# Polysketch attention with a routed two-layer expert network: more products of zeros at the start, and last output tiles in one plain transfer per queue

## The chip, the cores and the metric

The kernel runs on one core of a Trainium2 chip. Five engines work side by side: TensorE (PE in the profile; PEld is its weight load), VectorE (DVE), ScalarE (ACT), GpSimd (POOL) and SyncE (SP). SP issues most transfers, ACT and POOL some; sixteen DMA engines carry them. An SPq or ACTq row of the timeline is the issuing alone, not the transfer. The metric is the time of one execution in microseconds on the device; lower is better.

## The reference, cut to what matters

Two stages follow each other. The attention has 4 batches, 4 heads, 1088 positions and 32 elements a head. The expert network has 4352 tokens of 128, 8 experts with 1024 hidden elements, and two experts per token.

```python
a, b = S1 @ x, S2 @ x                     # 8 sketches each, for x = q and x = k
phi(x) = outer(a, b)                      # 64 features per position and head
kv = phi(k).T @ v;  z = phi(k).sum(0)
attn = phi(q) @ kv / (phi(q) @ z + 1e-6)  # [4, 1088, 4 heads * 32] = tokens x
noisy = x @ w_gate + log(1 + exp(x @ w_noise)) * noise
top2  = the two largest of 8, softmax weights
out[t] = sum over the token's two experts e of weight * (relu(x[t] @ w1[e]) @ w2[e])
```

## The kernel before, in words

**An order that is written out.** The kernel first makes a list of jobs: each has the engines that may run it, what it reads and writes, and a function that emits its instructions. `PLACES` is the order in which the jobs are emitted, `ENGINES` the engine of each, by its number. Each engine, SP's queue among them, takes its instructions in that order, so a waiting one holds up what is behind it. `HOLDS` ties a group of transfers to a scatter that must come first. `ZEROS` names the jobs ahead of which TensorE multiplies zeros: the number is how many products of 512 columns in bf16 (the last may be shorter). They write to a tile that nobody reads (`idle`, L471). Their operand is in fact a constant of ones; the text keeps the name.

**The first batch** (L626 and on). The matrices S are taken apart (L591 to L603) and turned (L568). Keys and queries are turned on VectorE (L614), multiplied by the sketches (L631, of 64 columns; L634, of 128), taken out of PSUM by ACT, and their outer products are made by VectorE or POOL (L666). When all tiles of keys are there, 72 products give kv (L748); from it come tokens, logits, routing and one-hot columns for the first experts.

**Routing.** For each call of the router a batch's tokens are weighed and scattered by POOL (L1084) into lists per expert in DRAM. With each row goes its pair number, 2 * token + choice, from the table `pid`, which `numbers` fills with iotas on POOL (L543 to L552) and L1047 copies next to the rows.

**The expert stage** (`block`). For each block of 128 or 256 rows of an expert, rows are fetched, turned, multiplied by w1 (L1195), rectified (L1203 on ACT, L1201 on VectorE), multiplied by w2 (L1210) and scattered to `pairs` in DRAM by their pair number (L1238). It begins near 37 us and lasts to the end; sketches and routing of later batches are put among it. The last two blocks are not scattered: their rows are given to the tokens by products with a matrix of ones and zeros, `spread` (L1219, L1228), which leaves sums in two PSUM banks, `late_acc`.

**The end** (`sums`, `in_tiles`). For each batch both rows of a token are loaded from `pairs` (`pr`), added on VectorE (L1268) and stored. A batch but the last has tokens in order on the partitions. In the last one the numbering is that of the tokens' places in the tiles: a partition holds position 32 * strip + t, a column is one of 9 tiles. The load is in that order as well, and the store has to undo it. Columns 0 to 3 are loaded and stored on SP before the last blocks are done. For columns 4 to 7 and for tile 8 the bank is added (L1274) before the store. `in_tiles` makes the targets: for columns below 8 there are two, one for each pair of strips, with extents [2 strips][32 t][columns][128]; partitions are 64 for each. Columns 4 to 7 are added and stored in two halves of two columns each, each half on SP and ACT. Tile 8 has two stores of 32 rows. `pr` and `o` have one buffer each. After the last store each engine reads `flag` and branches (L1484, L1486), to a part for lists that are too long, which isn't entered; then SP waits for all transfers.

Of the kernel before, what the change touches and what calls it, by code (L numbers as in the profile page):

```python
# [1518 lines left out]
```

## Time and profile before

| | |
|---|---|
| median of 3 runs | 352.35 us (350.09, 352.35, 353.89) |
| the profiled execution's own time | 354.55 us |
| its span, first to last instruction | 352.7 us |
| mean granted TensorE clock | 0.983 |
| PE busy | 333.4 us (95%), 2844 products |
| DVE / ACT / POOL busy | 176.6 (50%) / 121.9 (35%) / 237.5 (67%) |
| moved by DMA | 42.82 MB, mean 121 GB/s |

The page cuts the span into 40 slices of 8.8 us; a digit is the busy share in tenths. TensorE is at 9 from the second slice to the 38th with one 8, at 2 in the 39th and 0 in the last. The chain that ended last is empty on this page, so the end is read from the timeline. Line numbers are those of the kernel before; L356 and L349 are helpers that issue all plain transfers and all copies, so their operands tell them apart.

### The profile page before, as it was taken

To read this page: it belongs to the slowest core of one execution; us is meant where nothing else is said; L and a number is where in the kernel's file an instruction comes from. 1 tells how busy PE (TensorE), PEld (TensorE's weight loads), DVE (VectorE), ACT (ScalarE), POOL (GpSimd) and SP (SyncE) were. 2 spreads that over 40 slices of the span, in tenths; PEclk is the share of its full clock that TensorE was granted. 3 is DMA by queue.
4 is the path that set the end of the run, shared out by engine and by line. 5 is a ranking of instruction groups with operands and counts; after the bars stand their busy time and mean duration, and the time that the engine had idled before them with its cause. 6 is when DMAs were issued, how large, how long until landed. Compare 5 with 4: busy or idle time off the path is not lost.

```text
span 352.7 us, 8086 instructions
## 1 busy us (share of the span) xinstructions
PE 333.4 (95%) x2844; PEld 317.6 (90%) x2844; DVE 176.6 (50%) x659; ACT 121.9 (35%) x325; POOL 237.5 (67%) x386
## 2 busy tenths in 40 slices
PE   8999899999999999999999999999999999999920
PEld 4986899999999999999999999999999999999920
DVE  4548887875927675543766522443323333334120
ACT  1237767743455432614122453111112221222300
POOL 7434586986497897396858698893886788646100
PEclk9999999999999999999999999999999999999985
DMA  7728996953475664555324371142343151535510
GB/s 205 236 75 222 253 336 197 267 170 82 98 163 120 119 167 101 72 110 90 74 55 89 58 195 41 41 71 65 62 82 103 62 113 45 144 118 147 139 37 31
DMA packets 91656, 42.82 MB, mean 121 GB/s; under 512 B 67105, under 2 KB 85154, under 8 KB 91612
## 3 DMA queue, kind: packets, MB, share of 16 engines
q1 hardware_dynamic: 86872, 33.24, 42.0%
q0 software_dynamic: 4544, 8.89, 7.1%
q8 instruction: 23, 0.38, 0.5%
q14 instruction: 21, 0.17, 0.2%
q10 hardware_dynamic: 196, 0.15, 0.1%
HBM read 26.27 MB, written 16.17 MB: 120 GB/s over the span
## 4 chain that ended last, share of the span: by engine, by line


## 5 line engine op out<-in xcount | busy, mean ns | idle before, releaser
L1210 PE MATMUL acc<-w2s,h 128*128 128x128 f32 x1152 | 145.5, 276 | 0.0
L1195 PE MATMUL hp<-bT,w1s 128*128 128x128 f32 (+1 forms) x896 | 144.7, 306 | 0.4 <-ACT bT L349 0.4
L1210 PEld LDWEIGHTS acc<-w2s,h 128*128 128x128 f32 x1152 | 139.8, 192 | 2.5
L1195 PEld LDWEIGHTS hp<-bT,w1s 128*128 128x128 f32 x896 | 121.7, 191 | 5.5 <-ACT bT L349 0.5
L1203 ACT ACTIVATE h<-hp 128x512 f32<-128x512 f32 x100 | 59.5, 596 | 134.1 <-PE hp L1195 121.1
L1084 POOL DMA_INDIRECT xs<-xg,to x72 | 71.4, 991 | 36.1 <-issue 13.9
L1238 POOL DMA_INDIRECT pairs<-y,mine x70 | 68.9, 985 | 36.6 <-issue 10.5
L904 POOL MEMSET step<- 1x512 f32 x142 | 73.0, 514 | 0.0
L1201 DVE TENSOR_SCALAR h<-hp 128x512 f32<-128x512 f32 x44 | 30.3, 688 | 67.1 <-PE hp L1195 60.8
L349 ACT COPY y<-acc 128x128 f32<-128x128 f32 x46 | 11.9, 263 | 39.4 <-PE acc L1210 37.4
L1185 DVE STREAM_TRANSPOSE bT<-xb 128x128 f32<-128x128 f32 (+1 forms) x48 | 16.3, 345 | 8.9 <-PE hp L1195 5.2
L1056 ACT ACTIVATE xg<-x,g 128x128 f32<-128x128 f32 x57 | 18.5, 394 | 2.0 <-DVE g L1010 2.0
L349 DVE COPY y<-acc 128x128 f32<-128x128 f32 x24 | 6.8, 285 | 19.8 <-PE acc L1210 11.8
L810 PE MATMUL bank<-kvw,pT 128*128 128x98 f32 x128 | 16.5, 273 | 0.0
L810 PEld LDWEIGHTS bank<-kvw,pT 128*128 128x128 f32 x128 | 15.5, 192 | 0.1
L1268 DVE TENSOR_TENSOR o<-pr 128x512 f32<-128x512 f32 (+1 forms) x12 | 6.5, 552 | 11.7 <-DMA pr<-pairs 11.0
L666 POOL TENSOR_TENSOR phq<-ab 128x512 f32<-128x512 f32 (+1 forms) x5 | 5.3, 1067 | 8.8 <-DVE ab L648 8.8
L634 PE MATMUL bank<-sk,qTs 128*128 128x128 f32 x64 | 10.2, 300 | 0.0
L634 PEld LDWEIGHTS bank<-sk,qTs 128*128 128x128 f32 x64 | 9.1, 213 | 0.2 <-issue 0.2
L666 DVE TENSOR_TENSOR phq<-ab 128x512 f32<-128x512 f32 (+1 forms) x13 | 8.1, 620 | 0.1
L471 PE MATMUL turn<-const-bfloat16-1.0 128*128 128x512 bf16 (+2 forms) x22 | 7.2, 482 | 0.9 <-PEq L1502 0.9
L648 DVE TENSOR_TENSOR ab<-bank,lo 128x256 f32<-128x256 f32 (+2 forms) x17 | 6.4, 383 | 2.8 <-ACT lo L349 2.4
(182 smaller groups left out, 291.6 us busy)
## 6 DMA issues: line engine op xcount, KB each, us to landing
w1s<-in_moe_w_dram SPq DMA_DIRECT2D x8, 512.0 KB
w2s<-in_moe_w_dram SPq DMA_DIRECT2D x8, 512.0 KB
pr<-pairs SPq DMA_DIRECT2D x8, 512.0 KB
kq<-in_k_dram SPq DMA_DIRECT2D x4, 544.0 KB
kq<-in_q_dram SPq DMA_DIRECT2D x4, 544.0 KB
vld<-in_v_dram SPq DMA_DIRECT2D x16, 128.0 KB
xb<-xs SPq DMA_DIRECT2D x128, 16.0 KB
there<-phq SPq DMA_DIRECT2D x16, 128.0 KB
```

Of the source, the lines that this page charges most:

```text
L349: A.copy(o, i) if e == "ACT" else V.tensor_copy(o, i)
L634: T.matmul(ps.t[rows, 2 * W * i:2 * W * i + 2 * W], lhsT=lhsT, rhs=sk[:].rearrange("p c h x -> p (c h x)"), start=True, stop=True)
L810: T.matmul(ps2.t[:, c0:c0 + 2 * YW], lhsT=pT.t[:, at + P * (2 * i + a):at + P * (2 * i + a) + P], rhs=kvw.t[:, a, :], start=True, stop=True)
L904: job.fill = G.memset(step[:], 0.0)
L1056: A.activation(out=xg.t[:, i, c, 0:D], in_=x.t[:, c, :], func=AF.Copy, scale=B_["g"].t[:, i, c:c + 1])
L1084: ins = G.indirect_dma_start(out=xs[:], in_=xg.t[rows, i, t, :], in_offset=None, out_offset=bass.IndirectOffsetOnAxis(ap=to.t[rows, i, t:t ...
L1185: add("DVE", vec(P * n), lambda _: V.transpose(bT.t[:, 0:P * n], flat()), r=[xb], w=[bT], prio=TOP + u)
L1195: T.matmul(hp.t[:, P * n * i:P * n * (i + 1)], lhsT=w1s[:, e, P * (js * g + i):P * (js * g + i + 1)], rhs=bT.t[:, 0:P * n], start=True, st ...
L1201: V.tensor_scalar_max(h.t[:], hp.t[:], 0.0)
L1203: A.activation(out=h.t[:], in_=hp.t[:], func=AF.Relu)
L1210: T.matmul(acc.t[:, D * c:D * c + D], lhsT=h.t[:, P * (n * i + c):P * (n * i + c + 1)], rhs=w2s[:, e, j, :], start=(j == 0 and c == 0), st ...
L1238: ins = G.indirect_dma_start(out=pairs[:], in_=y.t[:], in_offset=None, out_offset=bass.IndirectOffsetOnAxis(ap=numbers_of[w].t[:, e, c:c + ...
```

## The change

Five things are edited, and with them the whole written order.

1. `ZEROS`: 4.5 products instead of 1.9 ahead of the first sketch; one product more ahead of the first product of queries with kv in the second router call. The 7.6 at the very start and the 12 stay (the job numbers move by one).
2. `numbers` no longer fills the last batch; `last_numbers` does, in twelve iotas. In columns 0 to 7 the number is now 8 * t + 2 * strip + choice plus the column's base, so a partition of the loaded sums is 4 * t + strip. In tile 8 it is 4 * t + 2 * strip + choice.
3. `in_tiles` gives targets with extents [16 t][4 strips][columns * 128] for columns below 8, two of them, of 64 partitions each; tile 8 has one target of 64 rows.
4. `sums` adds the bank once and stores each target once; the halves are gone. The products that give the last blocks' rows to columns 0 to 3 of the bank are one job instead of two.
5. `PLACES`, `ENGINES` and `HOLDS` are new. TensorE's own order is nearly the same (1.1 places of shift on average); on SP, ACT and VectorE jobs move by 7 to 14 places on average, and about 50 jobs change from VectorE to ACT or the other way. Near the start: the last query sketch comes ahead of the key products; the blank block `pad` is written early on POOL instead of after the query products; the transfers of the second batch and the weights are reordered, with the second weights of expert 0 seventh among the sixteen weight loads instead of second. `last_numbers` stands among the scatters of batch 2. At the end, SP's order is: the two stores of columns 0 to 3, the load of columns 4 to 7, the load of tile 8, a store of batch 2, the store of columns 4 to 7 (with ACT), the store of tile 8.

```diff
-HOLDS = {'clear5': (1, 4, 0), 'clear6': (8, 0), 'w2_7': (0, 1, 1), 'zeros': (5, 7, 0)}
+HOLDS = {'clear6': (1, 2, 1), 'v3': (1, 2, 1)}
...
-ZEROS = {43: 7.6, 49: 1.9, 152: 12}
+ZEROS = {44: 7.6, 50: 4.5, 153: 12, 222: 1}
@@ -549,8 +549,17 @@
                     if l < 2:
                         G.iota(pid[rows, i, 0:B - 1, C], pattern=[[2 * S, B - 1]], base=2 * (32 + l) + i,
                                channel_multiplier=2 * TN)
-                G.iota(pid[:, i, B - 1, :], pattern=[[2 * P, C + 1]], base=2 * S * (B - 1) + i, channel_multiplier=2)
-        pool_job(2.7, 15, numbers, ["pid"])
+        pool_job(2.5, 15, numbers, [("pid", 0)])
+
+        def last_numbers():
+            for i in range(2):
+                for l in range(4):
+                    rows = slice(32 * l, 32 * l + 32)
+                    G.iota(pid[rows, i, B - 1, 0:C], pattern=[[2 * P, C]], base=2 * S * (B - 1) + 2 * l + i, channel_multiplier=8)
+                    if l < 2:
+                        G.iota(pid[rows, i, B - 1, C:C + 1], pattern=[[2 * P, 1]], base=2 * (S * (B - 1) + P * C) + 2 * l + i,
+                               channel_multiplier=4)
+        pool_job(2.2, 250, last_numbers, [("pid", 1)], [("pid", 0)])
         pool_job(3.0, 26, lambda: limits(1, NW + 1), [("limits", 1)], ["base"])
         add("DVE", 0.3, lambda e: (V.tensor_copy(starts[:, 0, :], base[:]), V.memset(over[:], -1.0)),
             r=["base"], w=[("starts", 0), "over"], prio=45, port=1)
@@ -1045,7 +1054,7 @@
         indexed = dve(0.2 + 2 * vec(16 * n), index, ["first", "row"], ["f2", "at", "to"], late)
         xg, to = B_["xg"], B_["to"]
         pool_job(gps(18) + 0.1, prio, lambda: G.tensor_copy(xg.t[:, :, 0:n, D:XW].bitcast(I32), pid[:, :, b, t0:t0 + n].unsqueeze(3)),
-                 [(xg, 9)], ["pid"])
+                 [(xg, 9)], [("pid", b // (B - 1))])
         for i in range(2):
             for c0 in range(0, n, 3):
                 c1 = min(n, c0 + 3)
@@ -1222,13 +1231,13 @@
             add(EV, either(D), lambda en: copy(en, y[:], acc.t[:, 0:D]), r=[acc], w=[("late", late)], prio=TOP + u)
 
             behind_it = []
-            for cs in ((4,), (0, 1), (2, 3)):
+            for cs in ((4,), (0, 1, 2, 3)):
                 def given(_, cs=cs):
                     for c in cs:
                         T.matmul(late_acc[c // 4].t[:, D * (c % 4):D * (c % 4) + D], lhsT=spread.t[:, P * c:P * c + P], rhs=y[:],
                                  start=(late == 0 and c in (0, 4)), stop=(late == LATE - 1), skip_group_check=True)
                 behind_it = [add("PE", len(cs) * mm(D), given, lat=0.15, r=[spread, ("late", late)],
-                                 w=[(late_acc[cs[0] // 4], cs[0] % 4 // 2)], prio=p0 + 60, after=behind_it)]
+                                 w=[late_acc[cs[0] // 4]], prio=p0 + 60, after=behind_it)]
             return
         for c in range(n):
             y = new("y")
@@ -1268,18 +1277,13 @@
             add("DVE", vec(P * c), lambda e, t=t, o=o, rows=rows, c=c: V.tensor_tensor(
                 out=o.t[rows, 0:c, :], in0=t.t[rows, 0:c, 0, :], in1=t.t[rows, 0:c, 1, :], op=ALU.add),
                 r=[t], w=[o], prio=prio, port=1)
-            halves = [(0, c)] if bank is None or c == 1 else [(0, c // 2), (c // 2, c)]
-            for half, (c0, c1) in enumerate(halves):
-                if bank is not None:
-                    add("DVE", vec(P * (c1 - c0)), lambda e, o=o, rows=rows, c0=c0, c1=c1, bank=bank: V.tensor_tensor(
-                        out=o.t[rows, c0:c1, :], in0=o.t[rows, c0:c1, :],
-                        in1=bank.t[rows, c0 * D:c1 * D].rearrange("p (c d) -> p c d", d=D), op=ALU.add),
-                        r=[(bank, half)], w=[(o, half)], prio=prio)
-                for i, (d_, part) in enumerate(dsts):
-                    dma(queues[i % len(queues)],
-                        lambda d_=d_, c0=c0, c1=c1, cut=len(halves) > 1: d_[:, :, c0:c1, :] if cut else d_,
-                        lambda o=o, part=part, c0=c0, c1=c1: o.t[part, c0:c1, :], [(o, half)], [("out", (b, at, half, i))], prio,
-                        size=600.0 * (c1 - c0) * (part.stop - part.start))
+            if bank is not None:
+                add("DVE", vec(P * c), lambda e, o=o, rows=rows, c=c, bank=bank: V.tensor_tensor(
+                    out=o.t[rows, 0:c, :], in0=o.t[rows, 0:c, :],
+                    in1=bank.t[rows, 0:c * D].rearrange("p (c d) -> p c d", d=D), op=ALU.add), r=[bank], w=[o], prio=prio)
+            for i, (d_, part) in enumerate(dsts):
+                dma(queues[i % len(queues)], lambda d_=d_: d_, lambda o=o, part=part, c=c: o.t[part, 0:c, :], [o], [("out", (b, at, i))],
+                    prio, size=600.0 * c * (part.stop - part.start))
 
     def whole(b):
         r0 = S * b
@@ -1297,10 +1301,9 @@
         src = pairs_t[r0 + P * c0:r0 + P * c1].rearrange("(c p) k d -> p c k d", p=P)
         dst = out[r0:r0 + S, :].rearrange("(t n) d -> t n d", n=TN)
         if c0 == C:
-            return ([(src[0:HB], slice(0, HB))], [(dst[:, 32 + l:33 + l], slice(32 * l, 32 * l + 32)) for l in range(2)], 1,
-                    late_acc[1])
-        dst = dst[:, 0:32].rearrange("t (l c) d -> l t c d", l=4)[:, :, c0:c1, :]
-        return ([(src, slice(0, P))], [(dst[2 * l:2 * l + 2], slice(64 * l, 64 * l + 64)) for l in range(2)], c1 - c0,
+            return [(src[0:HB], slice(0, HB))], [(dst[:, 32:TN, :].unsqueeze(2), slice(0, HB))], 1, late_acc[1]
+        dst = dst[:, 0:32, :].rearrange("t (l c) d -> t l c d", c=C)[:, :, c0:c1, :]
+        return ([(src, slice(0, P))], [(dst[16 * i:16 * i + 16], slice(64 * i, 64 * i + 64)) for i in range(2)], c1 - c0,
                 late_acc[0] if c0 else None)
 
     late_acc = [new("bank"), new("bank")]
```

## Rows read from the trace of the kernel before

**Rows 1.** The page, part 2: busy tenths of PE and DMA in 40 slices.

```profile
PE   8999899999999999999999999999999999999920
...
DMA  7728996953475664555324371142343151535510
```

**Rows 2.** Windows: busy us by engine, granted clock, DMA share, GB/s.

```profile
40.00:60.00 20.00, 20.00 (x235) 19.13 (x234) 15.89 (x65) 14.77 (x43) 15.14 (x18) 1.00 1.00 278
250.00:300.00 50.00, 50.00 (x341) 46.92 (x340) 16.24 (x40) 10.16 (x22) 40.23 (x61) 1.00 0.31 78
```

**Rows 3.** Timeline from 330 us: start us, us, engine, line, operation, count.

```profile
329.63 0.69 DVE L1268 TENSOR_TENSOR o<-pr 128x512 f32<-128x512 f32 x1 [4.56 <-DMA pr<-pairs]
...
330.35 1.19 SPq L356 DMA_DIRECT2D out_dram<-o  x2
...
331.85 1.24 SPq L356 DMA_DIRECT2D pr<-pairs  x2
...
336.37 1.38 PE L1228 MATMUL bank<-late_y,blocks 128*128 128x128 f32 x10 [0.35 <-ACT late_y L349]
340.68 0.88 DVE L1268 TENSOR_TENSOR o<-pr 128x512 f32<-128x512 f32 x2 [5.85 <-DMA pr<-pairs]
341.67 0.94 DVE L1274 TENSOR_TENSOR o<-o,bank 64x128 f32<-64x128 f32 x3
341.97 1.64 SPq L356 DMA_DIRECT2D out_dram<-o  x3
341.98 1.91 ACTq L356 DMA_DIRECT2D out_dram<-o  x3
```

**Rows 4.** Windows over stretches near the end.

```profile
324.00:325.00 1.00, 1.00 (x11) 1.00 (x10) 0.86 (x4) 0.00 (x1) 0.34 (x1) 1.00 0.54 201
334.00:335.00 1.00, 1.00 (x12) 1.00 (x11) 0.55 (x1) 0.00 (x0) 0.00 (x0) 1.00 0.97 338
...
347.00:350.00 3.00, 0.00 (x0) 0.00 (x0) 0.00 (x0) 0.00 (x0) 0.00 (x0) 0.50 0.14 48
```

**Rows 5.** Lines 1484 and 1486: duration ns min/median/max, first and last start.

```profile
L1484 SPq TENSOR_LOAD <-flag x1: 1563/1563/1563, 343.7 to 343.7; - x1
...
L1486 SPq EVENT_SEMAPHORE  x8: 17/17/17, 345.8 to 350.6; - x8
...
L1486 SPq COMPARE_BRANCH  x1: 50/50/50, 345.3 to 345.3; - x1
```

**Rows 6.** Timeline of the first 30 us.

```profile
0.81 0.41 SPq L356 DMA_DIRECT2D words<-in_S_dram  x1
...
0.85 3.40 PE L471 MATMUL turn<-const-bfloat16-1.0 128*128 128x512 bf16 x8 [0.85 <-PEq L1502]
...
2.44 0.38 DVE L591 TENSOR_SCALAR expo<-words 16x32 uint32<-16x32 uint32 x1 [2.44 <-DMA words<-in_S_dram]
...
4.51 0.99 PE L471 MATMUL turn<-const-bfloat16-1.0 128*128 128x512 bf16 x2
...
6.08 3.67 PE L631 MATMUL bank<-sk,kTs 128*128 128x64 f32 x16 [0.57 <-DVE kTs L614]
...
19.07 4.06 PE L748 MATMUL acc<-phk,vaug 128*33 128x64 f32 x72
```

**Rows 7.** Line 471 in the first 6 us, duration ns min/median/max.

```profile
L471 PE MATMUL turn<-const-bfloat16-1.0 x10: 462/631/631, 0.9 to 4.9; 128*128 128x512 bf16 x8, 128*128 128x307 bf16 x1, 128*128 128x460 bf16 x1
```

**Rows 8.** Line 471 from 29 to 34 us.

```profile
L471 PE MATMUL turn<-const-bfloat16-1.0 x12: 379/381/383, 29.9 to 32.3; 128*128 128x512 bf16 x12
```

**Rows 9.** Window over the first batch's sketches.

```profile
5.50:20.20 14.70, 14.13 (x83) 14.01 (x84) 7.35 (x15) 3.12 (x10) 6.25 (x38) 1.00 0.85 240
```

**Rows 10.** Lines 550, 552 and 547, the pair numbers on POOL.

```profile
L550 POOL IOTA pid<- x4: 127/130/131, 7.3 to 8.7; 32x3 int32 x4
...
L552 POOL IOTA pid<- x2: 146/148/150, 8.2 to 9.3; 128x9 int32 x2
...
L547 POOL IOTA pid<- x8: 143/150/158, 7.2 to 9.1; 32x24 int32 x8
```

More of the change, by code (lines that the diff above doesn't have):

```diff
@@ L102 @@
 TURNED = (2, 3)
-HOLDS = {'clear5': (1, 4, 0), 'clear6': (8, 0), 'w2_7': (0, 1, 1), 'zeros': (5, 7, 0)}
-PLACES = [20, 21, 3, 33, 4, 42, 0, 25, 41, 26, 43, 44, 1, 47, 49, 56, 35, 50, 29, 30, 2, 55, 59, 60, 48, 52, 40, 16,
[73 rows of a table removed]
-ENGINES = (
-    "ASSSASSSGGGGGGSSSSSSGGGGGGGGGGGGGGGGGGGGGDDPDAADDPADPADDDDDPADPADPADPADPADPPPPPAAPAADPADGGPADGSSSSSSSSSSSSSSSS"
-    "SSSSSSSSSSSSSSSPAPDDDAPAPDDAAAAAADDDDDDDGAPDDGGDDGDAAADDGGGGGGGGSDDDAADPADGDDDDPADGGPADDDDPADGDPPPAAPAADPDDGDP"
-    "APDDPAPDDPAPDDAAAADDDDDDDDAPDDDGAAAADDGGGGGGGGGGPAPDDPAPDDAAAADDDDDDDDAPDDDGAAAADDGGGGGGGGPAPDDPAPDDPAPDDAAAAD"
-    "DDDDDDGAPDDDGAAAADDGGGGGGGGGGSSSSSSSSAADPDDDDDDDPDDDDPDDDDDPDDDDSSSSSSSSDPPPAAPAADPDDDDSSSSSSSSDPDDPDDPDDPDDPA"
-    "PDDAAAADDDDDDDDAPDDDGAAAADDDDGGGGGGGGGGGGGGGGGGSSSSSSSSAADPADDDDDDPADDDPDDDDDPADDDSSSSSSSSDPPPDDPAADPDDDDSSSSS"
-    "SSSDPDDPDDPDDPDDPAPDDAAAADDDDDDDDAPDDDGAADAADDDGGGGGGGGGGGGGGGGGGGSDDDDAPPPPAPAPPAPAGAAADPPPPAPAPPAPAGAAAAPPPP"
-    "DPAPPAPDGDAAAPPPPAPAPPAPAGSPAPAPPAPAGSPAPAPPAPAGSPDPAPPAPAGSPAPAPPAPAGSDDDSSSSDPAPPAPAGSSSSDPAPPAPAGSSSSDPAPPA"
-    "PAGSSSSDPAPPAPAGSSSSDPAPPAPAGSSSSDPAPPAPAGSSSSDPAPPAPAGSSSSDPAPPAPAGSDDDDDDSSSSDPAPPAPAGSSSSDPAPPAPAGSSSSDPAPP"
-    "APAGSSSSDPAPPAPAGSSSSDPDPPAPAGSSSSDPAPPDPDGSSSSDPAPPDPAGSSSSDPAPPAPAGSDSSDSSDSSDDDDDDSSSSDPAPPAPDGSSSSDPDPPAPA"
-    "GSSSSDPDPPDPAGSSSSDPAPPAPDGSSSSDPAPPAPAGSSSSDPDPPDPDGSSSSDPAPPDPDGSSSSDPAPPAPDGSSDDDDDDSSSSDPAPPDPPAPPAPAGDGSS"
-    "SSDPAPPAPPAPPAPDGAGSSSSDPAPPDPPAPPAPAGAGSSSSDPDPPAPPDPPAPDGDGSSSSDPDPPDPPDPPDPDGDGSSSSDPDPPAPPDPPAPDGAGSSSSDPA"
-    "PPDPPDPPAPDGAGSSSSDPAPPDPPDPPAPAGAGSDSSDSSDSSSDDDDDDSSSSDPDPPDPPAPPDPAGDGSSSSDPAPPDPPDPPAPAGDGSSSSDPDPPAPPDPPA"
-    "PDGAGSSSSDPDPPAPPDPPAPDGAGSSSSDPAPPDPPAPPAPAGDGSSSSDPDPPAPPDPPAPDGAGSSSSDPAPPDPPAPPDPAGDGSSSSDPDPPAPPDPPAPAGAG"
-    "SDSSDSSDSSDSSSDDDDDDSSSSDPDPPAPAGSSSSDPAPPAPAGSSSSDPDPPAPDGSSSSDPAPPAPAGSSSSDPAPPDPDGSSSSDPDPPDPAGSSSSDPAPPAPD"
-    "DPPPSSSSDPAPPAPDAPPPSDDSASDDSADSA")
@@ L194 @@
-ZEROS = {43: 7.6, 49: 1.9, 152: 12}
+HOLDS = {'clear6': (1, 2, 1), 'v3': (1, 2, 1)}
+PLACES = [4, 3, 20, 33, 42, 43, 44, 21, 45, 1, 48, 50, 0, 56, 60, 24, 57, 49, 53, 51, 35, 52, 18, 63, 2, 61, 62, 36,
[73 rows of a table added]
+ENGINES = (
+    "ASSSASSSGGGGGGSSSSSSGGGGGGGGGGGGGGGGGGGGGGDDPDAADDPADPADDDDDPADPADPADPADPADPPPPPAAPAADPADGGPADGSSSSSSSSSSSSSSS"
+    "SSSSSSSSSSSSSSSSPAPDDAAPAPDDDAAAAADDDDDDDGAPDDGGDDGDAAADDGGGGGGGGSDDDAADPADGDDDDPADGGPADDDDPADGDPPPAAPAADPDDGD"
+    "PAPDDPAPDDPAPDDAAAADDDDDDDDAPDDDGAAAADDGGGGGGGGGGPAPDDPAPDDAAAADDDDDDDDAPDDDGAAAADDGGGGGGGGPAPDDPAPDDPAPDDAAAA"
+    "DDDDDDDGAPDDDGADAADDGGGGGGGGGGSSSSSSSSAADPADDDDDDPDDDDPADDDDPDDDDSSSSSSSSDPPPDAPDDDPADDDSSSSSSSSDPDDPDDPDDPDDP"
+    "APDDAAAADDDDDDDDAPDDDGAAAADDDDGGGGGGGGGGGGGGGGGGSSSSSSSSAADPADDDDDDPADDDPADDDDPADDDSSSSSSSSDPPPDDPADDPDDDDSSSS"
+    "SSSSDPDDPDDPDDPDDPAPDDAAAADDDDDDDDAPDDDGADADDDDDGGGGGGGGGGGGGGGGGGGSDDDDAPPPPAPAPPAPAGDAADPPPPAPAPPAPAGAAAAPPP"
+    "PAPAPPAPAGDAAAPPPPAPAPPAPAGSPDPAPPAPAGSPAPAPPAPAGSPDPAPPAPAGSPAPAPPAPAGSDDDSSSSDPAPPAPAGSSSSDPAPPAPAGSSSSDPAPP"
+    "APDGSSSSDPAPPAPAGSSSSDPAPPAPAGSSSSDPAPPAPAGSSSSDPAPPAPAGSSSSDPAPPAPAGSDDDDDDSSSSDPAPPAPDGSSSSDPAPPAPAGSSSSDPAP"
+    "PAPAGSSSSDPAPPAPAGSSSSDPAPPAPAGSSSSDPAPPDPDGSSSSDPAPPDPDGSSSSDPAPPAPAGSDSSDSSDSSDDDDDDSSSSDPDPPDPAGSSSSDPDPPAP"
+    "AGSSSSDPDPPAPAGSSSSDPAPPAPAGSSSSDPAPPAPDGSSSSDPAPPAPAGSSSSDPAPPAPAGSSSSDPAPPAPAGSSDDDDDDSSSSDPDPPAPPAPPAPDGDGS"
+    "SSSDPAPPDPPDPPAPDGAGSSSSDPDPPAPPDPPDPAGAGSSSSDPDPPAPPDPPDPAGDGSSSSDPDPPAPPDPPDPDGAGSSSSDPAPPAPPAPPAPAGDGSSSSDP"
+    "APPAPPAPPAPAGDGSSSSDPAPPAPPAPPAPDGAGSDSSDSSDSSSDDDDDDSSSSDPAPPAPPAPPAPDGDGSSSSDPDPPDPPDPPAPDGAGSSSSDPAPPAPPAPP"
+    "DPAGAGSSSSDPAPPDPPAPPDPDGAGSSSSDPDPPAPPDPPDPAGAGSSSSDPDPPAPPAPPDPAGDGSSSSDPAPPAPPDPPDPAGAGSSSSDPDPPAPPDPPDPAGA"
+    "GSDSSDSSDSSDSSSDDDDDDSSSSDPAPPDPAGSSSSDPAPPDPAGSSSSDPDPPAPAGSSSSDPAPPAPAGSSSSDPAPPDPAGSSSSDPAPPAPAGSSSSDPDPPAP"
+    "DDPPSSSSDPAPPDPDAPPSDDSSDDSA")
```

146 rows, old and new, of the table PLACES are left out of this document.

## The prediction

> **What bounds the kernel now.** I read the page's slices first: TensorE is busy in nearly every one until the last two [rows 1]. Then the windows by stage: from 40 us to the end of the work TensorE is 100% busy, and no other engine comes near it [rows 2]. Its products in that stretch are the same ones after the change, so nothing done there by another engine counts unless TensorE is made to wait. What is left are the two ends, where TensorE is not saturated or not at full speed.
>
> **The end.** In the timeline [rows 3] the last product (L1228) ends at 336.37 + 1.38 = 337.75 us. The sum of the pairs (L1268) that is to be added to it starts only at 340.68, after 5.85 us of waiting for a load issued at 331.85. Then the adds run to 342.6 and the six stores are issued until 343.9, but the span goes on to 352.7. The windows say why [rows 4]: from 347 to 350 the sixteen DMA engines are busy 0.14 of the time at 48 GB/s, that is 0.14 x 16 = 2.2 engines. A store in which all take part has 0.54 and 201 GB/s in its microsecond (324 to 325), and loads reach 0.97 and 338 GB/s (334 to 335). So the stores of the last batch run on two engines or so, and their shape says which two: the outermost extent of their target is [2 strips]. The stores of columns 0 to 3, issued at 330.35, have the same shape, and they leave the queue of two engines full; the load issued at 331.85 has its share on these two behind them. That is the wait of 5.85 us.
>
> The Trainium skill ("DMA: Bandwidth & Descriptors", Why a DMA increments its semaphore by 16 and not by 1) states that a transfer uses the largest number of engines up to 16 that divides the slowest dimension of both sides: 2 before and 16 after. The 2.2 engines of the trace agree with the first; no row shows an outermost extent of 16.
>
> **The start.** The same product of zeros, 128x512 in bf16, takes 631 ns before 6 us [rows 7] and 381 ns after 29 us [rows 8]; eight of them start 0.43 us apart at first [rows 6]. 512 columns in 0.43 us are 1.2 GHz, the lower level. The granted clock is printed as 1.00 there, but its first record lies later, so it says nothing of the start. At 19.07 the 72 products of 64 columns still take 4.06 us (0.056 each, 1.2 GHz) [rows 6]; the clock rises between these and 29 us, although TensorE has been issuing since 0.85 with one gap of 0.57 us ahead of the first sketch at 6.08. All of the first batch's sketches, 12.9 us, and its key products, 3.9 us, are at the lower level.
>
> **The change, part by part.**
>
> *Stores of the last batch.* Both stores of columns 0 to 3 and both of columns 4 to 7 get an outermost extent of 16, with rows of 2 KB. I take it that all 16 engines carry them (the only other value is that of before, below). Columns 0 to 3 are 256 KB: at 201 GB/s 1.3 us instead of the time until the load lands at 340.6. The load of 576 KB behind them needs 1.7 us at 338 GB/s; issued at 331.85 to 333, it lands near 336 to 336.5 with about 1.2 us for landing (0.81 to 2.44 for a tiny load, less 0.41 of issue [rows 6], an estimate). So TensorE's 337.75 comes last, by more than a microsecond. From there: 0.1 to wake VectorE (estimate), one add of 128x512, for which I take the 0.69 of the same shape at 329.63 (the two halves of now take 0.94 with a third small add [rows 3]): 338.55. SP issues its store (1.64 / 3 = 0.55) until 339.1 and the small one of tile 8 until 339.65; ACT in parallel 0.64. The 256 KB land at 338.55 + 0.6 + 1.3 + 1.2 = 341.7. Behind its last store SP reads the flag (1.56), branches, and reaches its end waits 0.5 later [rows 5]: 341.7 as well. Eight waits without waiting are some 0.5, and from the last of them (350.6) to the end of the span it is 2.1 now: 344.3. The span ends 352.7 - 344.3 = **8.4 us earlier**. Bounds: 9.4 if the flag read costs only 0.5; 6.4 if the load or the spread stores come 2 us later than this.
>
> *One add and one spread product for two, one store fewer on ACT.* In the sum above; the products are the same four, so TensorE's 1.38 stays.
>
> *Pair numbers of the last batch.* Two iotas of 0.148 us leave the start and twelve of 0.13 to 0.15 come later [rows 10]: 1.7 us on POOL, put among the scatters of batch 2. Behind it are scatters whose rows are fetched much later; TensorE's 100% covers them. POOL is busy 40 of 50 us [rows 2], so it has room; price 0, and 1.7 if that cover were gone. Nothing reads the numbers before batch 3.
>
> *Products of zeros.* 4.5 for 1.9 at the first sketch: 2.6 x 0.43 = 1.1 us more at the lower level, of which 0.57 fills the gap: the first sketch starts 0.5 later. If the clock is still low, this goes through to the end, as TensorE sets this stage. The last query sketch (two products at 0.23 each [rows 6]) now stands ahead of the key products: 0.45. Together +0.9 (low end 0). The single product put in at the second place is 0.2 us in a stretch where TensorE waits for others; 0.
>
> *The clock.* What the added products may bring is that the clock rises before the first sketch. No row shows it. Ends: 0, and a gain bounded by VectorE, which is busy 7.35 us of 5.5 to 20.2 [rows 9]: this stretch can't shrink by more than 14.7 - 7.35 = 7.3. TensorE alone would give (12.9 + 3.9) / 2 = 8.4. I take 4: the executions of the unchanged kernel lie 4.5 us apart (350.09 to the profiled 354.55), though TensorE's stretch from 40 us has nothing in it that could vary by so much; a clock that rises at different moments would do it, and then the fastest is what an early rise gives. That is inferred, not shown. A reason for less than 7: the loads of the weights are the next to be late; the DMA engines are at 1.00 from 40 to 60 us [rows 2].
>
> The Trainium skill ("TensorE: Matmul & The Clock Gate", The HAM clock gate) holds that the slow clock is the default and activity releases it, and calls the loss by it under 1% of a typical span. By that figure the gain would be at most 3.5 us (an estimate) and the sum 342.7. The trace differs: at least 22 of 352.7 us, 6%, are at the lower level.
>
> **Sum.** The profiled execution took 354.55, 1.85 of it outside its span, 2.2 above the median of 352.35. 354.55 - 8.4 - 4 = **342.2**. Checked another way: the fastest, 350.09, less 8.4 is 341.7.
>
> **Rivals.**
> 1. The forecast, end and early clock: 342.2 (338.0 to 345). Chance 0.57.
> 2. The end alone; the clock rises where it did. For it: 17 us of nearly gapless sketches did not raise it. Against: those are small products behind long weight loads, the products of zeros are not. 354.55 - 8.4 + 0.9 = 347.1 (to 348). Chance 0.28.
> 3. The change doesn't do what it says: the stores stay on few engines. Against: the extents. The end then stays at 352.7 within 1, and with or without an early clock it comes to 350.5 to 355. Chance 0.05.
> 4. Slower: the whole order is new, and some transfers are no longer held back. In the new list the second weights of expert 0 are the seventh of sixteen weight loads instead of the second. If weights come after TensorE wants them in the first pass over the experts, 40 to 60 us, where the DMA engines have nothing to spare [rows 2], TensorE waits there. It decides from 10 us: 354.55 - 8.4 + 10 is 356, 1% over the median; at 278 GB/s that is 2.8 MB, five weight loads behind time. Against: before 26 us the engines are far from full [rows 1]. Time 357. Chance 0.04.
> 5. New waits of 1 to 5 us somewhere in TensorE's stretch, with the end as forecast: 344 to 350. Chance 0.06.
>
> **Range and chances.** About 1%, 3.5 us, is what a measurement can tell from no change. Low end: 354.55 - 9.4 - 7.3 = 337.9; high end 348, rival 2 with its bound. Left out are 3, 4 and part of 5. Faster by over 1% is below 348.8: 1, 2, and most of 5: 0.91. Within 1%: most of 3, some of 5: 0.05. Slower: 0.04.
>
> **What would show it.** Right: in the last stretch the sum of the pairs no longer waits after TensorE's last product; the windows between the last add and the end show a DMA share well over 0.14 for about a microsecond and no plateau at 48 GB/s; the span ends 6.5 to 7 us after the last product instead of 15. For the clock: the first sketches of 64 columns 0.11 us apart instead of 0.21, and the key products starting near 14 to 16 us. Wrong: a plateau at 48 GB/s (rival 3), key products at 20 us (rival 2), gaps in TensorE with a DMA as their releaser after 38 us (rival 4).

## The result and the profile after

The changed kernel took **340.13 us** (median of 4 runs, 339.66 to 342.71) against 352.03 us of the kernel before: a ratio of 0.968, 95% interval 0.961 to 0.975. Forecast were 342.2 us, 337.9 to 348.0. In every ratio here, runs more than 1.5% above the fastest of the same kernel are left out. The profiled execution took 339.91 us, its span 338.2. Lines behind the new function stand 3 to 9 further down: L1228 is now L1237, L1268 is L1277, L631 is L640, L748 is L757.

**The whole span.** The page's slices and two windows (us by engine, granted clock, DMA share, GB/s) answer to [rows 1] and [rows 2]:

```profile
PE   8997999999999999999999999999999999999991
...
DMA  7999994944563664465325166214534021323451
```

```profile
40.00:60.00 20.00, 19.35 (x230) 18.70 (x230) 14.14 (x63) 15.54 (x47) 16.96 (x22) 1.00 0.81 220
250.00:300.00 50.00, 50.00 (x346) 47.12 (x345) 16.87 (x38) 9.02 (x21) 36.84 (x50) 1.00 0.31 78
```

TensorE still fills the stretch between the two ends. From the first product with an expert's weights (L1204, `w1s`) to the end of the last product it is 299.71 us, from 31.80 to 331.51; before it was 300.00, from 37.75 to 337.75. Nothing was won or lost there.

**The end.** The timeline (start, us, engine, line, operation) and the windows answer to [rows 3] and [rows 4]:

```profile
326.49 0.99 SPq L356 DMA_DIRECT2D pr<-pairs  x2
327.52 6.22 SPq L356 DMA_DIRECT2D out_dram<-o  x3
...
330.13 1.38 PE L1237 MATMUL bank<-late_y,blocks 128*128 128x128 f32 x10 [0.35 <-ACT late_y L349]
331.01 0.69 DVE L1277 TENSOR_TENSOR o<-pr 128x512 f32<-128x512 f32 x1 [1.54 <-DMA pr<-pairs]
331.81 0.69 DVE L1281 TENSOR_TENSOR o<-o,bank 128x512 f32<-128x512 f32 x1
332.42 0.27 DVE L1277 TENSOR_TENSOR o<-pr 64x128 f32<-64x128 f32 x1
332.53 0.66 ACTq L356 DMA_DIRECT2D out_dram<-o  x1
```

```profile
333.00:334.00 1.00, 0.00 (x0) 0.00 (x0) 0.00 (x1) 0.00 (x0) 0.00 (x0) 1.00 0.20 66
334.00:335.00 1.00, 0.00 (x0) 0.00 (x0) 0.00 (x0) 0.00 (x0) 0.00 (x0) 1.00 0.74 236
335.00:336.00 1.00, 0.00 (x0) 0.00 (x0) 0.00 (x0) 0.00 (x0) 0.00 (x0) 0.73 0.04 10
336.00:338.20 2.20, 0.00 (x0) 0.00 (x0) 0.00 (x0) 0.00 (x0) 0.00 (x0) 0.50 0.00 0
```

The sum of the pairs now starts at 331.01, half a microsecond ahead of the end of the last product (331.51), where it started 2.93 us behind it. It ends at 331.70, so it is still the load, by 0.19 us, and not TensorE that comes last; the chain of work that ended last (start, us, what) runs through it:

```profile
326.49 4.40 DMA pr<-pairs
...
331.01 0.70 DVE o L1277
```

The plateau of 0.14 and 48 GB/s is gone: most of what the last stores move is moved in one microsecond, at 0.74 of all engines. From the last product to the end of the span it is 6.69 us instead of 14.99: **8.30 us**. What answers to [rows 5] (duration in ns, starts):

```profile
L1487 SPq TENSOR_LOAD <-flag x1: 807/807/807, 333.8 to 333.8; - x1
...
L1489 SPq EVENT_SEMAPHORE  x8: 17/17/17, 335.2 to 336.5; - x8
```

The flag's load costs 0.81 now, so SP reaches its end waits at 335.2 and stands in them until 336.5: the landing of the stores sets the end, 4.0 us behind the add that they carry (332.50).

**The start.** The timeline of TensorE answers to [rows 6] and [rows 7]; the windows are cut where the granted clock changes:

```profile
0.85 3.40 PE L471 MATMUL turn<-const-bfloat16-1.0 128*128 128x512 bf16 x8 [0.85 <-PEq L1505]
...
4.47 1.16 PE L471 MATMUL turn<-const-bfloat16-1.0 128*128 128x512 bf16 x5
5.67 2.00 PE L640 MATMUL bank<-sk,kTs 128*128 128x64 f32 x16
...
10.71 1.50 PE L640 MATMUL bank<-sk,qTs 128*128 128x64 f32 x8 [0.81 <-DVE qTs L623]
...
15.41 2.21 PE L757 MATMUL acc<-phk,vaug 128*33 128x64 f32 x72
```

```profile
4.40:11.20 6.80, 5.95 (x48) 5.07 (x47) 4.51 (x10) 1.01 (x4) 3.16 (x17) 1.00 1.04 208
11.20:14.60 3.40, 3.40 (x19) 3.40 (x18) 1.50 (x4) 1.57 (x4) 3.05 (x13) 0.50 1.01 327
14.60:18.00 3.40, 3.40 (x83) 3.15 (x82) 3.39 (x9) 0.98 (x5) 2.28 (x8) 1.00 0.92 278
```

Sixteen sketches of 64 columns take 2.00 us instead of 3.67, the 72 key products 2.21 instead of 4.06. The records of the granted clock, which began at 23.45 us in the profile before, begin at 4.37 here, fall to half at 11.20 and are full again from 14.61. The key products start at 15.41 instead of 19.07, and the last product ends at 331.51 instead of 337.75: **6.24 us**.

The twelve iotas of the last batch's pair numbers, in place of the two of [rows 10], ran at 153.6 to 155.3 us on POOL:

```profile
L558 POOL IOTA pid<- x8: 124/128/158, 153.6 to 155.2; 32x8 int32 x8
```

### The profile page after: what moved, and what is told of

It is laid out like the page before. It is cut to its first block, busy times and chain, and to the rows that moved or that the text cites. A ratio compares the mean times of both kernels' runs of the same rounds, so it can differ in the third digit from the quotient of the medians.

```text
span 338.2 us, 8094 instructions
## 1 busy us (share of the span) xinstructions
PE 326.5 (97%) x2848; PEld 311.4 (92%) x2848; DVE 174.4 (52%) x652; ACT 121.8 (36%) x325; POOL 239.6 (71%) x396
## 4 chain that ended last, share of the span: by engine, by line
PE 73%; DMA 8%; POOL 7%; issue 5%; DVE 4%; SPq 1%; ACT 1%; POOLq 0%; DVEq 0%
PE hp L1204 30%; PE acc L1219 29%; POOL pairs L1247 5%; PE bank L819 4%; PE bank L643 4%; POOL step L913 2%; DMA out_dram<-o 2%; DMA kq<-in_q_dram 2%; PE bank L757 2%; SPq L356 1%; DMA pr<-pairs 1%; PE turn L1165 1%; DMA xb<-xs 1%; PE bank L807 1%; DVE o L1277 1%
## 5 line engine op out<-in xcount | busy, mean ns | idle before, releaser
L1204 PE MATMUL hp<-bT,w1s 128*128 128x128 f32 (+1 forms) x896 | 145.5, 306 | 0.1
L1204 PEld LDWEIGHTS hp<-bT,w1s 128*128 128x128 f32 x896 | 121.2, 192 | 5.0 <-ACT bT L349 0.4
L1212 ACT ACTIVATE h<-hp 128x512 f32<-128x512 f32 x104 | 62.0, 598 | 122.2 <-PE hp L1204 107.4
L1247 POOL DMA_INDIRECT pairs<-y,mine x70 | 69.7, 996 | 34.7 <-ACT y L349 18.2
L1210 DVE TENSOR_SCALAR h<-hp 128x512 f32<-128x512 f32 x40 | 27.7, 691 | 74.0 <-PE hp L1204 52.8
L349 ACT COPY y<-acc 128x128 f32<-128x128 f32 x52 | 13.2, 265 | 41.7 <-PE acc L1219 36.4
L1065 ACT ACTIVATE xg<-x,g 128x128 f32<-128x128 f32 x49 | 16.0, 394 | 0.0
L349 DVE COPY y<-acc 128x128 f32<-128x128 f32 x18 | 5.0, 282 | 18.7 <-PE acc L1219 18.1
L1277 DVE TENSOR_TENSOR o<-pr 128x512 f32<-128x512 f32 (+1 forms) x12 | 6.5, 544 | 7.7 <-DMA out_dram<-o 6.1
L675 DVE TENSOR_TENSOR phq<-ab 128x512 f32<-128x512 f32 (+1 forms) x13 | 9.3, 717 | 0.1
L349 ACT COPY pT<-bank 128x512 f32<-128x512 f32 (+1 forms) x12 | 6.2, 516 | 4.5 <-PE bank L807 4.4
```

Of the source, the lines that this page charges most:

```text
L349: A.copy(o, i) if e == "ACT" else V.tensor_copy(o, i)
L1065: A.activation(out=xg.t[:, i, c, 0:D], in_=x.t[:, c, :], func=AF.Copy, scale=B_["g"].t[:, i, c:c + 1])
L1204: T.matmul(hp.t[:, P * n * i:P * n * (i + 1)], lhsT=w1s[:, e, P * (js * g + i):P * (js * g + i + 1)], rhs=bT.t[:, 0:P * n], start=True, st ...
L1210: V.tensor_scalar_max(h.t[:], hp.t[:], 0.0)
L1212: A.activation(out=h.t[:], in_=hp.t[:], func=AF.Relu)
L1247: ins = G.indirect_dma_start(out=pairs[:], in_=y.t[:], in_offset=None, out_offset=bass.IndirectOffsetOnAxis(ap=numbers_of[w].t[:, e, c:c + ...
```

## The experiments

For the end there were two theories: **A**, the outermost extent of the target sets how many DMA engines carry a store; **B**, it is the new order and the merging of the halves. For the start also two: **C**, the 2.6 added products of zeros raise the clock early; **D**, the first eight do it as well, as the execution has it, and the order of the start does the rest. The first four kernels ran on one chip, the next four and the last four on another, in two groups at different times. The kernel before was run in each group: 355.12 us in the median (348.62 to 356.40) in the first, 349.65 in the second (346.20 to 353.60, and one run of 864.35 that nothing here explains), 351.93 in the third (347.66 to 355.11). Kernels of one group are compared with each other; the changed kernel itself is in the second and third group alone.

**The old shape of the target in the changed kernel** (strips outermost, [2 strips][32][4][128], with the numbers to match):

```
-  base=2 * S * (B - 1) + 2 * l + i, channel_multiplier=8)
+  base=2 * S * (B - 1) + 64 * l + i, channel_multiplier=2)
-  rearrange("t (l c) d -> t l c d", c=C)   ... dst[16 * i:16 * i + 16]
+  rearrange("t (l c) d -> l t c d", c=C)   ... dst[2 * i:2 * i + 2]
```

> The kernel after with one thing undone: in columns 0 to 7 of the last batch the pair numbers again follow the strips, and the stores have extents [2 strips][32 t][columns * 128] instead of [16 t][4 strips][columns * 128]; order, counts of instructions, zeros and the merged stores stay as after. Theory A (the outermost extent sets how many DMA engines carry a store, and the load behind them waits for the two): the end grows back by about 8 us, to 347 to 349; from 4 us before the end to the end of the stores a DMA share near 0.14 at 48 GB/s, and the last sum of pairs waits several us for its load. Theory B (the end became shorter by the new order of SP's queue and by one merged store per queue): no change, 340 within 1.

Measured: 353.48 us (351.48 to 355.07), near the time of the kernel before, with the whole new order left in. That is 4.5 to 6.5 us over what Theory A expected: the end grew by 9.9 us instead of 8, on a chip where the kernel before took 3 us longer. Timeline and windows of its end:

```profile
331.68 1.38 PE L1237 MATMUL bank<-late_y,blocks 128*128 128x128 f32 x10 [0.35 <-ACT late_y L349]
337.04 0.69 DVE L1277 TENSOR_TENSOR o<-pr 128x512 f32<-128x512 f32 x1 [6.01 <-DMA pr<-pairs]
...
338.55 0.66 ACTq L356 DMA_DIRECT2D out_dram<-o  x1
```

```profile
340.00:345.00 5.00, 0.00 (x0) 0.00 (x0) 0.00 (x0) 0.00 (x0) 0.00 (x0) 0.50 0.20 42
345.00:348.00 3.00, 0.00 (x0) 0.00 (x0) 0.00 (x0) 0.00 (x0) 0.00 (x0) 0.50 0.08 32
```

Both marks of before are back: the wait for the load of the pairs (6.01 us) and the slow plateau (42 and 32 GB/s). The last product ends at 333.06, and it is 16.58 us from there to the end. A holds; what B may be worth is in the next run.

**The stores alone, in the kernel before** (its own order and zeros; the numbers of the last batch and the target as in the change, the two halves kept):

```
-  G.iota(pid[:, i, B - 1, :], pattern=[[2 * P, C + 1]], ..., channel_multiplier=2)
+  for l in range(4):
+      G.iota(pid[32 * l:32 * l + 32, i, B - 1, 0:C], pattern=[[2 * P, C]],
+             base=2 * S * (B - 1) + 2 * l + i, channel_multiplier=8)
+  ...
-  rearrange("t (l c) d -> l t c d", l=4)   ... dst[2 * l:2 * l + 2]
+  rearrange("t (l c) d -> t l c d", l=4)   ... dst[16 * l:16 * l + 16]
```

> The kernel before with the numbering and the store targets [16 t][4 strips] in columns 0 to 7 alone: the old order, two halves per store, tile 8 and the zeros as before; the twelve small iotas stand at the start in place of two. Theory A: the end is about 8 us shorter, 343 to 345, a little more than the merged stores take because of two more stores. Theory B: 352 within 1.

The edit has ten iotas at the start, not the twelve that the expectation names. Measured: 346.32 us (343.21 to 349.12), 1.3 over the 343 to 345 expected and 8.8 under the kernel before in this group. Timeline and windows of its end (L1271, L1231 and L1277 here are the sum, the last products and the adding of the bank):

```profile
332.32 0.89 DVE L1271 TENSOR_TENSOR o<-pr 128x512 f32<-128x512 f32 x2 [0.93 <-DMA pr<-pairs]
332.95 1.38 PE L1231 MATMUL bank<-late_y,blocks 128*128 128x128 f32 x10 [0.35 <-ACT late_y L349]
...
334.37 0.75 DVE L1277 TENSOR_TENSOR o<-o,bank 128x256 f32<-128x256 f32 x2 [0.61 <-PE bank L1231]
```

```profile
336.00:337.00 1.00, 0.00 (x0) 0.00 (x0) 0.00 (x0) 0.00 (x0) 0.00 (x0) 0.61 0.49 161
337.00:338.00 1.00, 0.00 (x0) 0.00 (x0) 0.00 (x0) 0.00 (x0) 0.00 (x0) 0.50 0.31 102
```

The wait of several us and the plateau are gone in the old order too. It is 7.08 us from the last product to the end, 0.39 more than with merged halves. So the extent gives 7.9 of the 8.3 us, and the merging with the new order 0.4. In this profile the clock was up from 5.13 us although the zeros are those of before: a first sign against C.

**The zeros alone, in the kernel before:** `49: 1.9` becomes `49: 4.5`.

> The kernel before with 4.5 products of zeros ahead of the first sketch instead of 1.9, nothing else. Theory C: the key products start at 15 to 16 instead of 19, and the time falls by 4 to 6 us, to 346 to 348. Theory D: 352 within 1.5, the first sketch 0.4 later where the clock is low.

Measured: 352.10 us (350.78 to 353.06), 3.0 under the median of the kernel before in this group and inside its spread. The profile shows an early rise (5.35) and key products at 13.34 instead of 19.07, but a last product that ends at 337.19, only 0.56 us earlier than before. More than 5 us were given back: the clock was at half again from 29.24 to 36.07, which costs up to 3.4, and TensorE has two waits of 1.62 and 1.06 us at 117 and 51 us, the second with nothing shown to release it, that neither of the first two profiles has. So the early rise that Theory C expects is there, and the gain in time that goes with it is not.

**The zeros of before in the changed kernel:** `50: 4.5` becomes `50: 1.9`. It ran in the first group and again in the third, there beside the changed kernel itself.

> The kernel after with 1.9 products of zeros ahead of the first sketch instead of 4.5. Theory C (the added products raise the clock before the first sketch, and the head is 6 us shorter for it): most executions take 345 to 347, and in the profile the sketches of 64 columns stand 0.21 us apart. Theory D (the clock's rise at 4.37 us in the profile after came before the added products began at 4.47, so the first eight can raise it by themselves, and the order of the head does the rest): 340 to 342, with as many early rises as the kernel after has.

> The changed kernel with the 1.9 products of zeros of before instead of 4.5 ahead of the first sketch, for the first time beside the changed kernel itself. Theory C (the longer run of zeros is what raises the clock early): in this profile, or in part of its times, the clock rises late, as without any zeros: 341 to 343. Theory D (the first eight do it as often): within 1 us of the changed kernel, or 0.5 faster by the shorter wait.

> The changed kernel a third time, as the measure for the next three on the same chip. From its first two profiles: clock up between 4 and 6 us, 16.4 us from the first key product to the first product of w1, 6.7 to 6.8 us behind the last product; 338 to 341.

Measured: 343.22 us (342.29 to 344.02) in the first group, between the ranges of the two theories. In the third 341.27 (338.65 to 346.57) beside the changed kernel's 340.46 (339.27 to 343.24), ratios to the kernel before of 0.972 (0.966 to 0.978) and 0.973 (0.967 to 0.979). The clock was up from 5.38 and 5.34. By the times the 2.6 products more are not to be told from none.

**No zeros at the start, zeros in the middle of it, and both parts in the old order**, beside the changed kernel in the second group:

```
after again    ZEROS = {44: 7.6, 50: 4.5, 153: 12, 222: 1}
no first       ZEROS = {153: 12, 222: 1}
midway         ZEROS = {44: 7.6, 50: 4.5, 72: 3, 153: 12, 222: 1}
both, old order: the kernel of "the stores alone" with ZEROS = {43: 7.6, 49: 4.5, 152: 12}
```

> The changed kernel again, unaltered, beside the kernel before on the same chip as the next three, so that they can be compared with it. Theory D (the moment at which the clock rises belongs to the execution; the order of the head does the rest): median 340 to 343, a last product near 331 to 335, 6.7 to 7.1 us behind it. Rival C (the longer run of zeros fixes the rise): the clock rises between 4 and 6.5 us in this profile too, falls for no longer than 3.5 us, and the median is 339.5 to 341.

> The changed kernel without the thirteen products of zeros ahead of the first sketch (the later ones stay). If those products are what lets the clock rise early, the key products start near 19 us instead of 15.4 and the last product comes 4 to 6 us later: 344 to 347. If a head at half speed is made good later (the order of the new head alone is worth the gain), the last product comes within 2 us of that of the changed kernel: 340 to 343.

> The changed kernel with three more products of zeros where TensorE waits 0.81 us for the first query tile (10 us), just ahead of where its clock fell to half at 11.20. If the small gap is what lets the clock fall, the clock stays at full speed from its rise on, the key products start near 14 instead of 15.4, and the time is 338.5 to 340.5. If the fall does not hang on that gap, the products cost what they overrun the gap by (3 x 0.22 - 0.81, nothing, up to 0.5 at half speed) and the time is that of the changed kernel within 1 us.

> The kernel before, in its own order of instructions, with both parts of the change at once: 4.5 products of zeros ahead of the first sketch and the new numbering and target of the last batch's stores (two halves kept). Apart they gave 3.0 (zeros) and 8.8 us (stores) of the 12 or so of the whole change. If the two parts add up and the new order brings nothing of its own, 340 to 343.5, the same as the changed kernel within 1.5. If the new order is what carries an early head through to the last product, 344 to 347, with a last product 3 us or more later than the changed kernel's.

Measured: the changed kernel 338.14 us (337.31 to 339.71; ratio to before 0.973, 0.968 to 0.977); no first zeros **343.06** (342.55 to 346.42; 0.989, 0.982 to 0.995); midway 339.30 (338.36 to 340.09); both in the old order **341.36** (338.57 to 343.47; 0.981, 0.976 to 0.985). The changed kernel is below both of its expected ranges.

Without the first zeros the time is 4.9 us longer, with no overlap of the runs (344 to 347 were expected; here the changed kernel itself is 2 us faster than in the first result). TensorE's timeline without them:

```profile
5.37 3.67 PE L640 MATMUL bank<-sk,kTs 128*128 128x64 f32 x16 [1.23 <-DVE kTs L623]
...
18.28 2.21 PE L757 MATMUL acc<-phk,vaug 128*33 128x64 f32 x72
```

and with them, in the changed kernel again:

```profile
5.79 1.89 PE L640 MATMUL bank<-sk,kTs 128*128 128x64 f32 x16
...
12.80 2.21 PE L757 MATMUL acc<-phk,vaug 128*33 128x64 f32 x72
...
24.74 0.18 PE L1009 MATMUL bank<-mk,earlier 128*128 128x32 bf16 x1 [0.65 <-DVE mk L992]
...
26.98 0.46 PE L1165 MATMUL turn<-blocks,x 128*128 128x128 f32 x2 [0.86 <-DVE blocks L1159]
```

Sketches at half speed (3.67 us for sixteen, as in [rows 6]) against full speed, and a rise at 17.55 against 5.13. The key products are 5.5 us apart, the ends of the last products 5.58: a late clock is not made good.

The products midway do not help: in this profile the clock stayed up from 6.47 on, but so it did in the changed kernel's second profile without them. Nor was there anything to fill: the second and third profiles of the changed kernel don't have the wait of 0.81 us at all. Whether it let the clock fall in the first is open.

Both parts in the old order are 3.2 us slower than the changed kernel: the time lies where it was expected if the parts add up, and yet not within 1.5 us of the changed kernel. In the profile of that kernel the key products are 0.91 us later than the changed kernel's, the stretch from there to the first `w1s` product takes 19.07 us instead of 16.40, and the last product ends 6.08 later. That pair is the slowest of seven runs beside the fastest of six, so it shows where time can go and not how much goes there in the median. Its timeline and a window:

```profile
27.62 0.18 PE L1003 MATMUL bank<-mk,earlier 128*128 128x32 bf16 x1 [2.36 <-ACT lo L349]
...
30.78 1.65 PE L1159 MATMUL turn<-blocks,x 128*128 128x128 f32 x6 [1.26 <-DVE blocks L1153]
```

```profile
31.00:34.00 3.00, 2.65 (x11) 2.35 (x12) 2.72 (x13) 1.47 (x5) 1.12 (x2) 0.50 1.25 265
```

In the old order TensorE waits 2.36 and 1.26 us here, in the new one 0.65, 0.86 and 0.47. The 2.36 belongs to this profile: the other three of the old order have 0.65, 0.65 and 1.16 in its place, so the waits of the old order are not longer as a rule. During the second wait the clock fell, and it was at half from 30.20 to 37.03. Six of its seven runs have a mean granted clock of 0.981 to 0.987, as the profile (0.984); the seventh has 0.995 and took 338.57 us, what the changed kernel takes. So what the new order is worth here seems to be mostly that the clock falls less often at 30 us: in the old order without such a fall (the stores alone) the same stretch took 16.65 us against 16.40. That is argued from these means and one profile; why the new order keeps the clock up more often is not shown.

**The single product at the second place, and the waits there filled**, beside the changed kernel in the third group: `222: 1` taken out; `153: 12, 222: 1` made `153: 14, 222: 4`.

> The changed kernel without the single product of zeros at the second place (27 us, among the waits for the first blocks). In the order of before, which has none there and waits up to 2.4 and 1.26 us in this stretch, the granted clock fell to half at 29.2 to 30.2 in two profiles with an early rise. If the single product keeps the clock up, a fall near 27 to 33 us shows here and costs 1 to 3 us. If not, the time is that of the changed kernel within 0.5.

> The changed kernel with two more products of zeros ahead of the wait of 0.65 us at 27 us and three more where the wait of 0.86 us follows. If waits in this stretch let the clock fall in some executions (mean clock 0.981 to 0.991 against 0.995 to 0.997), all executions now keep it up and the median is 0.3 to 1.5 us below the changed kernel's. If the added products come in the way of what waits behind them, it is 0.3 to 1.0 us above.

Measured: without the single product 340.04 us (338.00 to 343.67; ratio to before 0.970, 0.963 to 0.977), with the waits filled 341.06 (338.19 to 343.60; 0.974, 0.968 to 0.979), the changed kernel 340.46. TensorE's timeline and a window without the single product:

```profile
27.98 1.65 PE L1165 MATMUL turn<-blocks,x 128*128 128x128 f32 x6 [0.47 <-DVE blocks L1159]
```

```profile
28.00:31.00 3.00, 3.00 (x12) 2.67 (x13) 2.69 (x14) 1.14 (x4) 1.33 (x2) 0.50 1.11 264
```

and with the waits filled (0.65 and 0.86 us become 0.21 and 0.22, 0.47 stays):

```profile
25.14 0.18 PE L1009 MATMUL bank<-mk,earlier 128*128 128x32 bf16 x1 [0.21 <-DVE mk L992]
...
28.31 0.94 PE L1165 MATMUL turn<-blocks,x 128*128 128x128 f32 x6 [0.47 <-DVE blocks L1159]
```

```profile
28.00:31.00 3.00, 2.55 (x20) 2.31 (x21) 2.72 (x14) 1.68 (x5) 1.66 (x3) 1.00 1.15 278
```

Without the product the clock fell (28.01 to 31.42), the same six products of 128 columns take 1.65 instead of 0.94 us, and four of six runs have a mean clock of 0.987 or 0.988; with the waits filled no run is below 0.991 (which is also what the changed kernel's first profile has, with one fall). The changed kernel itself lies between, with three of six at 0.986 to 0.990. The clock also fell with the product in place (the zeros of before, 29.28 to 32.69), and four of six is not to be told from three of six. The medians don't follow either: all three lie within 1.1 us, and each kernel's runs are 4 to 6 us apart. No version beats the changed kernel.

**When the clock rose**, by the first record in each profile (us; "end" is that of the last product, "behind" from there to the end of the span):

| kernel | rise | half again | first key product | first w1s product | end | behind |
|---|---|---|---|---|---|---|
| before (1.9) | 23.45 | | 19.07 | 37.75 | 337.75 | 14.99 |
| after (4.5) | 4.37 | 11.20 to 14.61 | 15.41 | 31.80 | 331.51 | 6.69 |
| after again | 5.13 | | 12.80 | 29.20 | 328.71 | 6.75 |
| after, third | 6.29 | | 14.45 | 30.90 | 332.30 | 6.70 |
| strips outermost (4.5) | 6.19 | | 14.23 | 30.69 | 333.06 | 16.58 |
| zeros alone (4.5) | 5.35 | 29.24 to 36.07 | 13.34 | 31.20 | 337.19 | 14.15 |
| stores alone (1.9) | 5.13 | 8.54 to 15.37 | 16.12 | 32.77 | 334.33 | 7.08 |
| zeros back (1.9) | 5.38 | 29.28 to 32.69 | 13.17 | 30.65 | 335.44 | 6.86 |
| zeros back, again (1.9) | 5.34 | | 12.63 | 29.64 | 331.92 | 6.55 |
| no first zeros (none) | 17.55 | | 18.28 | 35.31 | 334.29 | 6.83 |
| midway (4.5) | 6.47 | | 14.44 | 30.89 | 331.45 | 6.81 |
| both, old order (4.5) | 6.30 | 30.20 to 37.03 | 13.71 | 32.78 | 334.79 | 6.97 |
| no single (4.5) | 4.12 | 28.01 to 31.42 | 12.82 | 29.98 | 330.24 | 6.39 |
| waits filled (4.5) | 5.65 | | 13.16 | 29.60 | 330.05 | 6.35 |

With 4.5 products the rise was early in all nine profiles, with 1.9 in three of four. In two of the nine it came at 4.12 and 4.37, before the products of the second group began (4.41 and 4.47), when only the eight ahead of them had run, which both kernels have. Every early rise came before the last of the products ahead of the first sketch had ended. With 1.9 they end at 5.4 to 5.5 us, and no rise came between 5.38 and 23.45; with 4.5 they end at 5.6 to 6.6, and five of the nine rises came at 5.65 to 6.47.

## Why the prediction was right, and where it was off

| term of the sum | predicted | profile before to profile after |
|---|---|---|
| from the last product to the end of the span | -8.4 (-6.4 to -9.4) | -8.30 |
| start: the clock, taken at | -4 (0 to -7.3) | -6.24 |
| outside the span | 0 | -0.1 |
| time | 354.55 to 342.2 | 354.55 to 339.91 |

**The end** went as its steps said. The stores are spread, at 236 GB/s where 201 were taken; the load of the pairs is no longer held up behind them; the span ends 6.69 us behind TensorE's last product, where 6.5 to 7 was said. One step did not hold: "TensorE's 337.75 comes last, by more than a microsecond". The load lands at 330.89, only 0.62 us ahead of the end of the last product, and the step left out the 0.69 us of the sum itself, which ends 0.19 behind that product. In six more profiles of the new order and target it ends 0.14 to 0.39 behind it; only without the single product and with the waits filled does TensorE come last. Inside the sum small sizes were off and cancel: for that reason the add ends 0.99 instead of 0.80 us behind the last product, SP's last wait follows 4.0 instead of 3.65 later, and then it is 1.7 instead of 2.1 to the end. The flag's load, 0.81 and not 1.56, no longer decides: SP has to wait for the stores behind it. The cause is shown and not only argued: the old extent brings back both marks with everything else new (16.58 us), the new one takes them away with the order old (7.08).

The Trainium skill ("DMA: Bandwidth & Descriptors", Why a DMA increments its semaphore by 16 and not by 1) has the number of engines as the largest up to 16 that divides the slowest dimension of both sides. These runs agree, as far as a share can tell: extent 2 gives 0.14 of sixteen engines before and 0.08 to 0.20 when put back, extent 16 gives 0.74, or 11.8 of the sixteen.

**The clock** was the right mechanism at the start of the profile pair; its size was off. The term was "I take 4", argued from the spread of the runs before; the profile pair has 6.24. As forecast for an early rise, the key products start between 14 and 16 (in the two later profiles of the changed kernel at 12.80 and 14.45). The 6.24 consist of 3.66 up to the first key product, 2.29 from there to the first `w1s` product (1.85 of that are the key products, at half speed before), and 0.29 behind. What was called inferred is now shown: with the clock late in the changed kernel the last product ends 5.58 us later and the time is 4.9 longer. Against the median of the runs of before the start brings less, 352.03 - 340.13 - 8.30 = 3.6, close to the 4: the profiled execution of before, at 354.55, is one with a late rise. That 4 was met is in part luck. In the second group the new order, with both other parts the same, is worth 3.2 us in the median, a term that the sum did not have, and the zeros to which the prediction gave the 4 show no gain in time that stands clear of the spread.

**What raises it** stays open. "What the added products may bring is that the clock rises before the first sketch" is not shown by the times: 1.9 in place of 4.5 cost nothing that can be measured in the new order, and 4.5 in the old kernel gave 3.0 us, inside the spread of the kernel before. The first eight can do it, and early rises come with 1.9 as well, so the added products are not needed in every execution. But the five rises at 5.65 to 6.47 came where only the kernels with 4.5 still multiply zeros, and where the clock had not risen by their end, or without any, it rose at 23.45 and 17.55. That speaks for the prediction in part of the executions. Whether the added products make a late rise rarer (none in nine profiles, against one in four) these numbers can't settle.

The Trainium skill ("TensorE: Matmul & The Clock Gate", The HAM clock gate) puts the penalty of the clock's ramp under 1% of a typical span. Here a late rise alone, with the zeros taken out, costs 4.9 of 338 us, 1.4%. The 6% that the prediction set against that figure is time at the lower level and not loss.

**The order of the start** was a term that the sum did not have, beyond 0.45 for the query sketch. It is worth 3.2 us in the median beside the same two parts in the old order; by the profiles the place is 25 to 31 us, where the clock falls less often in the new order. "The single product at the second place; 0" holds for the time (340.04 without it, 340.46 with it); for the clock nothing can be told.

**What was costed at nothing:** the pair numbers (1.6 us of POOL at 154 us, under TensorE's 299.71 us, against 300.00 before) and the spread products cost nothing. The zeros' half microsecond of delay did not come: with the clock up, 4.5 products end earlier than 1.9 did at half speed (first sketch 5.67 instead of 6.08).

**The rivals.** "The end alone" (347.1) is what the stores alone gave, 346.32, on another chip. Stores that don't spread (350.5 to 355) are what the old extent gives, 353.48. New waits in TensorE's stretch did not come in the pair (300.00 us from the first `w1s` product before, 299.71 after), but the stretch took 301.40 in the third profile of the changed kernel and 304.79 with the zeros of before. Late weights did not come: after 32 us TensorE waits for no transfer, only once for 0.7 us with nothing shown to release it and for 0.35 at the end; from 40 to 60 us the DMA engines have 0.81 instead of 1.00 [rows 2].

**Open** are three things: how often the clock of the kernel before rises late (the mean granted clock can't tell, as it takes the time ahead of the first record for full speed: it is 0.983 in the profile with the late rise, and in the second group runs with 0.981 to 0.985 took 346.2 to 353.6 us); why the runs of one kernel differ where their mean clocks hardly do (338.2 to 341.9 us at 0.993 to 0.997 with the waits filled); and short waits of TensorE with nothing shown to release them. In the first profile of the kernel with the zeros of before:

```profile
46.52 0.32 PE L757 MATMUL bank<-phk,vaug 128*33 128x64 f32 x3 [0.37 <-issue]
47.29 0.29 PE L757 MATMUL bank<-phk,vaug 128*33 128x64 f32 x2 [0.46 <-issue]
```

They can be missing records as well as waits.

## What to carry to other kernels

Read the DMA share of the last microseconds: here a plateau far below one, with nothing else running, was a store on few engines, and the remedy was the order of the dimensions of its target, even though the numbering of the rows had to be changed for it. Such a store also held back the load queued behind it, so its cost showed first as a wait for a load. A granted clock is that of one execution: compare several profiles before a product of zeros, or its number, is given the credit.
